# One head pair's output weights loaded in three pieces on a four-engine split, and smaller edits of loads and order, in a one-core decode kernel

## The chip, the cores and the metric

The kernel runs on one core of one Trainium2 chip. A core has TensorE (PE, matrix products; PEld is its weight load), VectorE (DVE), ScalarE (ACT), GpSimd (POOL), SyncE (SP, which here only issues transfers), and 16 DMA engines that move data from the chip's memory (HBM) into the on-chip memory. The engines run side by side and wait for one another by semaphores. The metric is device time of one execution in microseconds (us), lower is better; it is the median of several executions. One more execution was recorded by the hardware profiler, and all rows below come from it.

## The reference

One decode step of a block with adaptive layer norms: four sequences (B = 4), one token each, width 512, all in float32. `c` gives six modulation terms; attention reads caches of 4096 keys and values for 8 key heads (four query heads each); then an MLP over a token axis of length 1 with 1792 hidden units.

```python
mod = (silu(c) @ w_mod).reshape(4, 6, 1, -1)
sa, ca, ga, sb, cb, gb = (mod[:, i] for i in range(6))
h = layernorm(x) * (1 + ca) + sa
x = x + ga * attention(h, k_cache, v_cache, wq, wo)   # softmax(q k^T / sqrt(128)) v, then @ wo
h = layernorm(x) * (1 + cb) + sb
x = x + gb * mixer(h, w1, b1, w2, b2)                 # w2 . gelu(w1 h + b1) + b2 for each channel
```

The inputs are 157 MB, nearly all of it keys and values, and each byte is used once.

## The kernel before, in words

**Units.** There are 32 units, one for each (sequence, key head) pair. Unit i needs a key tile (128 rows, 16 KB each, 2 MB in all) and a value tile of the same size. For each unit PE makes the scores (`scores`, L221), DVE their row maximum, PE and DVE turn it and spread it over the rows, ACT takes the exponential (L251), DVE transposes the probabilities, PE multiplies them with the values (`values`, L281), the groups are picked and scaled (`pick`, `copy_o`), and the result goes through the unit's output weights (`project`, L332) into an accumulator per sequence.

**Loads.** All input loads are issued by SP in program order. `load_pair(i)` (L166) loads the keys of unit i + 2 and the values of unit i in one transfer of 4 MB into a ring of three slots (`tag="kv"`); it waits until the slot that it overwrites has been read. The output weights lie in four tiles of two heads each, `wo_p[0]` to `wo_p[3]`, each 128 rows of 16 KB, loaded by `load_wo` (L171) at the start and in the iterations 1, 3 and 5 of the main loop. `load_wm24` (L175, L176) loads three of the modulation matrices in two transfers, `load_wm5` the sixth at the end. The last unit's values come by `load_v` in pieces: a list `cuts` gives the column blocks (32 blocks `j` of 128 numbers per row) at which a piece ends. A transfer of 128 rows is shared among the 16 DMA engines.

**Order.** The engines run their instructions in the order in which the program issues them (`manual_schedule`). For units 0 to 23 a loop sets it; for the last eight units it is written out by hand, in `PLAN`, one word a step: `v31.2` is the third part of the last unit's value products, `z31` the last two column blocks of them (L299), `a31`, `A31`, `p31` pick, scale and project it. The words that start with z are the end of the last sequence: statistics of the attention's result (`zs`), their gathering over the rows by a product with ones (`zg`, L372 and L377), modulation (`zm`), broadcast (`zb0`, `zb1`, L411) and normalisation (`zn`).

**Mixer.** For each sequence a `Mixer` expands the normalised row to 14 blocks `js` (DVE, L425), applies gelu (ACT, L481) and contracts them with `w2` (`contract_wide`, L436: one block uses one strip of 32 of PE's columns, so that four blocks use all four strips). Sequence 2's mixer runs beside the last eight units; two of its last contractions (`c`) stand in the plan after the gather of the last sequence. The last sequence's own mixer is `finish` (L527): ACT and DVE alternate over the 14 blocks, PE contracts each, and in between PE makes the last gate (`modmm`, L199) from the sixth modulation matrix in four steps k, of which step 0 is made by `zw0` ahead of it.

Lines that set the places:

```python
cuts = {NS - 1: (0, 16, 24, 28, 30, 32), NS - 2: (0, 16, 32)}
last, halves = [(0, 1, 2, 3), (4, 5), (6,), (7,)], [(0, 1), (2, 3), (4, 5), (6, 7)]
... E x v31.0 f v31.1 v31.2 v31.3 V31 z31 a31 I A31 p31
zs g zq zg T2 c zx c zm zq zb0 T3 zg zb1 zw0 zn zc
```

`WIDE` (L24) says how many copies of the four picked columns `pick` writes for units 27 and 28: a product with 4 x that many columns of which only four are used.

Of the kernel before, what the change touches and what calls it, by code (L numbers as in the profile page):

```python
# [14 lines left out]
B, D, HQ, HKV, SK, DH, F = 4, 512, 32, 8, 4096, 128, 1792  # L15
REP = HQ // HKV
NF = F // 128
EPS = 1e-5
P = 128
NS = B * HKV  # L20
NSM = 3 * NF + 16 + 1


WIDE = {NS - 5: 24, NS - 4: 32}  # L24
NARROW = NS - 3


@with_exitstack
def adaln_decode(ctx: ExitStack, tc: tile.TileContext, small, x, wmod, wq, kk, kv, vv, wo, out):
    nc = tc.nc  # L30
    pad = ctx.enter_context(tc.tile_pool(name="pad", bufs=1))
    ring = ctx.enter_context(tc.tile_pool(name="ring", bufs=3))
# [13 lines left out]
    sm = cst.tile([P, NSM], F32, name="sm")  # L46
    xr = wk.tile([P, D], F32, name="xr", tag="yw", bufs=1)[0:B]
    wm01 = ring.tile([P, 2, 4, D], F32, name="wm01", tag="kv")
    nc.sync.dma_start(wm01, wmod[0])
    nc.sync.dma_start(sm, small)  # L50
    nc.sync.dma_start(xr, x)
    wqt = []
    for k in range(0, 4, 2):
        t = ring.tile([P, 2, HQ * DH], F32, name=f"wq{k}", tag="kv")
# [28 lines left out]
    wo_p = [wos.tile([P, 2, REP, D], F32, name=f"wo{h}") for h in range(0, HKV, 2)]  # L83
# [65 lines left out]
    def slots():  # L149
        return ring.tile([P, 2, SK], F32, name="kv", tag="kv")  # L150
# [17 lines left out]
        value(t[:, 1], i)  # L168

    def load_wo(h):  # L170
        nc.sync.dma_start(wo_p[h // 2], wo[h // 2])  # L171

    def load_wm24():
        w = ring.tile([P, 3, 4, D], F32, name="wm24", tag="kv")
        nc.sync.dma_start(w[:, 0:2], wmod[1])  # L175
        nc.sync.dma_start(w[:, 2], wmod[2][:, 0])  # L176
        for e in range(3):
            WM[2 + e] = w[:, e]

    def load_wm5():  # L180
        t = slots().rearrange("p s (k n) -> p (s k) n", n=D)
        nc.sync.dma_start(t[:, 0:4], wmod[2][:, 1])
        WM[5] = t[:, 0:4]
        return t[:, 4:6]

# [10 lines left out]
    def modmm(pm, t, ks=range(4)):  # L196
        for k in ks:
            for c in range(4):
                mm(pm[32 * c:32 * c + 32, :], sT8[:, k].rearrange("p b r -> p (b r)"),  # L199
                   WM[t][:, k, c * P:(c + 1) * P], start=(k == 0), stop=(k == 3))  # L200
# [107 lines left out]
    def pick(i):  # L308
        po = PV.pop(i)
        n, m = po.shape[-1] // DH, WIDE.get(i, 1)  # L310
        if i in OT:
# [38 lines left out]
    def fold_groups(pool, acc, tag):  # L350
        pc = pool.tile([P, P], F32, name="pc", tag=tag)
        for c in range(4):
            mm(pc[32 * c:32 * c + 32, :], first, acc[:, c * P:(c + 1) * P], start=True, stop=True)
        return pc
# [68 lines left out]
    def expand(u, hb, wr, js):  # L423
        for e, j in enumerate(js):
            dv.tensor_scalar(u[:, e, :], hb, wr[:, j:j + 1], b1[:, j:j + 1], op0=OP.mult, op1=OP.add)  # L425

    def contract(py, u, js):
        for e, j in enumerate(js):
            for c in range(4):
                mm(py[32 * c:32 * c + 32, :], w2[:, j:j + 1].to_broadcast([P, 32]),  # L430
                   u[:, e, c * P:(c + 1) * P], start=(j == 0), stop=(j == NF - 1))

    def contract_wide(py, u, js):
        for e, j in enumerate(js):
            q = j % 4
            mm(py[32 * q:32 * q + 32, :], w2[:, j:j + 1].to_broadcast([P, 32]), u[:, e, :],  # L436
               start=(j < 4), stop=(j >= NF - 4))

    class Mixer:
# [48 lines left out]
        def consume(self, most=9):  # L488
# [3 lines left out]
                (contract_wide if self.wide else contract)(self.py, u, js)  # L492
            del self.done[:most]

        def gather_up(self):
            yw = wk.tile([P, D], F32, name="yw", tag="yw", bufs=1)
            dv.tensor_copy(yw, self.py)
            self.py = fold_groups(ps_e, yw, "e")
# [27 lines left out]

    def finish(b, pg, py, hb, wr):  # L527
        uu = ring.tile([P, 16, D], F32, name="uu", tag="kv")
        for js in ((0,), (1,), (2, 3, 4), (5, 6, 7), (8, 9, 10), (11, 12), (13,)):
            j = js[0]  # L530
            if j < 2:
                nc.scalar.activation(uu[:, j], hb, AF.Gelu_apprx_tanh, bias=b1[:, j:j + 1], scale=wr[:, j:j + 1])
                u = uu[:, j:j + 1]
            else:
                u = uu[:, j:j + len(js)]
                expand(u, hb, wr, js)
                nc.scalar.activation(u, u, AF.Gelu_apprx_tanh)  # L537
            contract(py, u, js)
            if j == 1:
                modmm(pg, 5, (1, 2, 3))  # L540
        mix.close()
        dv.tensor_mul(osb[:, :B - 1], ZK, pg.unsqueeze(1).to_broadcast([P, B - 1, P]))
        dv.tensor_add(osb[:, :B - 1], osb[:, :B - 1], XK[:, :B - 1])
        gbl = cst.tile([P, P], F32, name="gbl")
        dv.tensor_copy(gbl, pg)
        dst = out.rearrange("b (c n) -> b c n", c=4)
        for e in range(B - 1):
            (nc.scalar if e == B - 2 else nc.sync).dma_start(dst[e], osb[8 * e:P:32, e])
        dv.scalar_tensor_tensor(osb[:, b], py, b2, gbl, op0=OP.add, op1=OP.mult)
        dv.tensor_add(osb[:, b], osb[:, b], XK[:, b])  # L550
        nc.sync.dma_start(dst[b], osb[8 * b:P:32, b])
# [15 lines left out]
    load_first()  # L567
    load_pair(0)
    load_wo(0)
    for i in range(2):  # L570
        for step in (scores, row_max, turn_max, col_max, spread_max, copy_max, expo):
# [3 lines left out]
    mix = None  # L575
    for i in range(NS - HKV):
        load_pair(i + 1)
        if i in (1, 3, 5):
            load_wo(i + 1)
        if i == 1:  # L580
            load_wm24()
# [17 lines left out]
        if i and i % HKV == 0:  # L599
            mix = Mixer(i // HKV - 1)  # L600
# [14 lines left out]
        if i == NS - HKV - 2:  # L615
# [4 lines left out]
    mix, row = Mixer(B - 2), Mixer(B - 1)  # L620
    pve = pgx = pc = ep = spare = slot = None
    gates = list(range(2 * REP))
    cuts = {NS - 1: (0, 16, 24, 28, 30, 32), NS - 2: (0, 16, 32)}
    last, halves = [(0, 1, 2, 3), (4, 5), (6,), (7,)], [(0, 1), (2, 3), (4, 5), (6, 7)]
    PLAN = """
    a23 v24.0 A23 p23 t25.0 P23 F R v24.1 LP25 G s26 t25.1 M H V24 LP26 Q a24 S26 v25.0 N s27 x A24 f p24 g
    x LP27 m26 S27 P24 m27 X26 X27 b26 B26 e26 x b27 v25.1 c g t26.1 l25 t26.0 B27 s28 V25 c g L25
# [1 line left out]
    LK30 t27.1 S29 P26 v27.0 m29 l27 g LK31 T t28.1 X29 LT t28.0 s30 L27 S30 b29 v27.1 B29 e29 l28 m30 V27  # L629
    LV28 L28 a27 g X30 t29.1 t29.0 l29 L29 s31 A27 LV29 b30 p27 x B30 S31 c c m31 e30 P27 X31 v28.0 f LT LV30  # L630
    b31 v28.1 B31 f e31 LV31 l30 V28 L30 t30.1 l31 L31 a28 t31.1 A28 p28 v29.0 v29.1 t30.0 f P28 V29 v30.0 a29
    v30.1 A29 LW p29 f v30.2 v30.3 t31.0 P29 g V30 Y y a30 A30 p30 E x v31.0 f v31.1 v31.2 v31.3 V31 z31 a31 I A31 p31
    zs g zq zg T2 c zx c zm zq zb0 T3 zg zb1 zw0 zn zc
    """
    TABLE = {"s": scores, "S": row_max, "m": turn_max, "X": col_max, "b": spread_max, "B": copy_max, "e": expo,
             "l": sums, "L": scale, "V": copy_v, "a": pick, "A": copy_o, "P": add_up,
             "LP": load_pair}
    MIX = {"F": mix.fold, "R": mix.residual, "G": mix.gather, "M": mix.modulate, "H": mix.gather, "Q": mix.spread,
           "N": mix.normalise, "g": mix.gelu, "c": lambda: mix.consume(1), "zc": mix.gather_up, "zq": row.gather_eps,
           "zg": row.gather,  # L640
           "zm": row.modulate, "zn": row.normalise}
    for step in PLAN.split():
        op, k = step.rstrip("0123456789."), step.lstrip("abcdefghijklmnopqrstuvwxyzABCDEFGHIJKLMNOPQRSTUVWXYZ")
# [22 lines left out]
        elif op == "LV":  # L666
            load_v(slot[:, i % 2], i, cuts.get(i, (0, 32)))
        elif op == "LW":
            spare = load_wm5()
        elif op == "x":  # L670
            mix.expand(spare if mix.n == 6 else None)
# [24 lines left out]
        elif op == "zb":  # L696
            if i == 0:
                py = ps_s.tile([P, 8, P], F32, name="py3", tag="s")
            row.spread(py[:, 4:], (2 * i, 2 * i + 1))
    finish(B - 1, pgx[:, 0], py[:, 0], row.hb, row.wr)  # L700


# [32 lines left out]
```

## Time and profile before

| | |
|---|---|
| median of 3 timed executions | 387.23 us (387.15 to 387.37) |
| the profiled execution | 387.3 us, of which the span shown is 385.2 |
| busy share: PE, DVE, ACT, POOL | 77%, 51%, 29%, 2% |
| loaded from HBM | 157.32 MB |
| mean granted clock of TensorE | 0.892 |

A row of the timeline gives start and duration in us, the engine, the kernel's line, the operation, output<-inputs by the program's names, shapes, how many, and in brackets how long the engine had been idle and which engine and line ended that. A row of the chain of waits gives start, duration and what the end was waiting for. L numbers are lines of the kernel before. A DMA share of 1.00 means that all 16 engines were busy.

### The profile page before, as it was taken

How to read it: one execution, taken by the hardware profiler on the slowest of the kernel's cores; microseconds unless marked ns; L12 is line 12 of the kernel's file. 1: busy time of each engine (PE TensorE's matmuls, PEld its weight loads, DVE VectorE, ACT ScalarE, POOL GpSimd, SP SyncE). 2: the span in 40 equal slices, each digit the busy share in tenths (PEclk: the TensorE clock that was granted, in tenths of full speed). 3: DMA queues.
4: the chain of work that ended last, by engine and by line, in shares of the span. 5: the costliest groups of instructions: out<-in, count | busy, mean ns of one | idle time of the engine just before them, and what ended most of it. 6: DMA issues, size and time to landing. Idle time of an engine off the chain costs nothing.

```text
span 385.2 us, 5574 instructions
## 1 busy us (share of the span) xinstructions
PE 295.1 (77%) x2376; PEld 116.2 (30%) x2376; DVE 195.4 (51%) x386; ACT 111.5 (29%) x141; POOL 8.5 (2%) x30
## 2 busy tenths in 40 slices
PE   0865778865856939879877868799777897999984
PEld 0111122311223303334322322343222353344653
DVE  0120252620442614664766545648665566788756
ACT  1001111121110111112567211115674103758166
POOL 1200000000000000000000000000000000000000
PEclk9998555985995886998999998989999998999999
DMA  8999999999999999999999999999999999999920
GB/s 331 436 436 436 407 456 436 407 439 429 423 444 432 424 436 432 434 436 434 436 435 436 434 433 430 425 429 427 432 434 432 430 432 424 432 423 427 416 101 3
DMA packets 7408, 157.68 MB, mean 409 GB/s; under 512 B 964, under 2 KB 1236, under 8 KB 1496
## 3 DMA queue, kind: packets, MB, share of 16 engines
q1 hardware_dynamic: 7376, 157.33, 95.2%
q8 instruction: 18, 0.29, 0.3%
q14 instruction: 6, 0.05, 0.0%
q10 hardware_dynamic: 8, 0.00, 0.0%
HBM read 157.32 MB, written 0.01 MB: 408 GB/s over the span
## 4 chain that ended last, share of the span: by engine, by line
DMA 54%; PE 32%; DVE 8%; ACT 4%; issue 1%; POOL 1%; SPq 0%; ACTq 0%
DMA kv<-in_kv 42%; PE s L221 10%; PE pv L281 7%; DMA wm<-in_wmod 5%; DMA kv<-in_kk 4%; DVE m L226 3%; PE s L113 2%; DVE p L257 2%; DMA sm<-in_small 2%; PE pa L332 2%; PE pt L318 1%; PE pb L241 1%; ACT uu L537 1%; PE pm L205 1%; PE pve L293 1%; PE pm L230 1%
## 5 line engine op out<-in xcount | busy, mean ns | idle before, releaser
L221 PE MATMUL s<-kv,QT 128*32 128x512 f32 x512 | 79.0, 745 | 42.1 <-DMA kv<-in_kv 38.5
L226 DVE TENSOR_REDUCE m<-s 128x1 f32<-128x1024 f32 x32 | 39.2, 1224 | 101.9 <-PE s L221 101.7
L251 ACT ACTIVATE p<-s,nm 128x1024 f32<-128x1024 f32 x32 | 35.6, 1114 | 182.7 <-DVE nm L246 182.6
L281 PE MATMUL pv<-kv,p 128*32 128x512 f32 x464 | 67.1, 646 | 0.5 <-DMA kv<-in_kv 0.5
L221 PEld LDWEIGHTS s<-kv,QT 128*32 128x32 f32 x512 | 16.5, 126 | 88.5 <-DMA kv<-in_kv 54.8
L318 PEld LDWEIGHTS pt<-g,po 128*128 128x128 f32 x236 | 30.4, 200 | 28.5 <-issue 21.2
L332 PE MATMUL pa<-wo,oT 128*32 128x512 f32 x240 | 33.6, 633 | 4.6 <-DVE oT L324 4.5
L318 PE MATMUL pt<-g,po 128*128 128x4 f32 (+2 forms) x236 | 33.1, 264 | 1.5 <-DVE po L304 1.0
L257 DVE STREAM_TRANSPOSE p<-p 128x1024 f32<-128x1024 f32 x25 | 30.8, 1233 | 0.0
L304 DVE COPY po<-pv 128x512 f32<-128x512 f32 x29 | 20.0, 688 | 15.5 <-PE pv L281 15.5
L235 DVE TENSOR_REDUCE mx<-pm 1x128 f32<-1x512 f32 x32 | 21.3, 669 | 1.1 <-PE pm L230 1.1
L425 DVE TENSOR_SCALAR u<-hb,wr,sm 128x512 f32<-128x512 f32 x40 | 19.9, 539 | 1.9 <-POOL wr L420 1.0
L481 ACT ACTIVATE u<-u 128x1024 f32<-128x1024 f32 x20 | 20.4, 1051 | 1.5 <-DVE u L425 1.4
L251 ACT ACT_TABLE_LOAD x11 | 14.1, 1283 | 20.4 <-DVE nm L246 20.4
L348 DVE TENSOR_TENSOR acc<-acc,pa 128x512 f32<-128x512 f32 x26 | 17.8, 686 | 3.1 <-PE pa L332 3.1
L241 PEld LDWEIGHTS pb<-neg,mx 1*128 1x128 f32 x64 | 10.0, 194 | 26.9 <-DVE mx L235 25.2
L113 PE MATMUL s<-wm,sT 128*4 128x512 f32 x16 | 9.0, 725 | 11.3 <-DVE sT L99 11.3
L481 ACT ACT_TABLE_LOAD x13 | 16.7, 1283 | 0.2
L281 PEld LDWEIGHTS pv<-kv,p 128*32 128x32 f32 x464 | 13.3, 146 | 6.2 <-issue 2.3
L230 PE MATMUL pm<-ident,m 128*1 128x128 f32 x32 | 9.2, 286 | 7.6 <-DVE m L226 3.5
L241 PE MATMUL pb<-neg,mx 1*128 1x1 f32 x64 | 12.7, 265 | 2.1 <-DVE mx L235 2.1
L436 PE MATMUL py<-u,sm 128*32 128x512 f32 x80 | 13.5, 593 | 0.4 <-ACT u L481 0.4
(134 smaller groups left out, 207.9 us busy)
## 6 DMA issues: line engine op xcount, KB each, us to landing
kv<-in_kv SPq DMA_DIRECT2D x28, 4096.0 KB, 21.9
wq<-in_wq SPq DMA_DIRECT2D x2, 4096.0 KB, 16.2
wo<-in_wo SPq DMA_DIRECT2D x4, 2048.0 KB
kv<-in_kv SPq DMA_DIRECT2D x4, 2048.0 KB, 19.5
wm<-in_wmod SPq DMA_DIRECT2D x2, 2048.0 KB, 14.4
kv<-in_kk SPq DMA_DIRECT2D x1, 4096.0 KB
kv<-in_vv SPq DMA_DIRECT2D x3, 1024.0 KB
wm<-in_wmod SPq DMA_DIRECT2D x1, 1024.0 KB
```

The costliest lines, as they stand in the source:

```text
L221: mm(s[32 * c:32 * c + 32, n * 512:(n + 1) * 512], QT[:, b, h, :], KT[i][:, (n * 4 + c) * 512:(n * 4 + c + 1) * 512], start=True, stop=True)
L226: dv.tensor_reduce(M[i], S[i], axis=AX.X, op=OP.max)
L235: dv.tensor_reduce(mx, M[i].rearrange("o (c r) -> o r c", c=4).unsqueeze(1).to_broadcast([1, 4, 32, 4]), axis=AX.X, op=OP.max)
L241: mm(pb, M[i].rearrange("o c r -> o (c r)"), neg1, start=True, stop=True)
L251: nc.scalar.activation(p, S[i], AF.Exp, bias=M.pop(i), accum_out=l)
L257: dv.transpose(PL[i][0], PL[i][0])
L281: mm(PV[i][32 * q:32 * q + 32, :], pT[:, 128 * k:128 * k + 128:4], VT[i][:, 4 * k:4 * k + 4, :].rearrange("p j d -> p (j d)"), start=(k < ...
L304: dv.tensor_copy(PV[i], pv)
L318: mm(pt, po[:, c * DH:(c + 1) * DH], sel.unsqueeze(1).to_broadcast([P, m, REP]), start=(c == 0), stop=(c == n - 1))
L332: mm(pa[32 * g:32 * g + 32, :], oT[:, g:g + 1].to_broadcast([P, 32]), wo_t[h][:, g, :], start=True, stop=True)
L425: dv.tensor_scalar(u[:, e, :], hb, wr[:, j:j + 1], b1[:, j:j + 1], op0=OP.mult, op1=OP.add)
L481: nc.scalar.activation(u, u, AF.Gelu_apprx_tanh)
```

## The change

Four groups of edits. (1) The third tile of output weights, `wo_p[2]`, is loaded by three transfers: the first 14 KB of each of the 128 rows, then the last 2 KB of the rows 0 to 123, then the last 2 KB of the rows 124 to 127. The host lays the weights out in four arrays for that. (2) Three modulation matrices come in one transfer in place of two, and the last unit's values in four pieces in place of five: the blocks 24 to 27 and 28, 29 are one piece, and their products one step. (3) Of sequence 2's remaining contractions the first block is made by a new step `k` ahead of the last sequence's first gather. (4) `finish` makes step 1 of the gate product ahead of its first contraction, and `pick` writes 32 copies for unit 27 in place of 24.

```diff
-WIDE = {NS - 5: 24, NS - 4: 32}
+LONG = 2 * 4 * 512 - 512
+WIDE = {NS - 5: 32, NS - 4: 32}
...
     def load_wo(h):
-        nc.sync.dma_start(wo_p[h // 2], wo[h // 2])
+        if h != HKV - 4:
+            nc.sync.dma_start(wo_p[h // 2], wo[h // 2] if h < HKV - 4 else w6)
+            return
+        flat = wo_p[h // 2].rearrange("p e g n -> p (e g n)")
+        nc.sync.dma_start(flat[:, :LONG], ws)
+        for lo, hi in ((0, P - 4), (P - 4, P)):
+            nc.sync.dma_start(flat[lo:hi, LONG:], wl[lo:hi])
 
     def load_wm24():
         w = ring.tile([P, 3, 4, D], F32, name="wm24", tag="kv")
-        nc.sync.dma_start(w[:, 0:2], wmod[1])
-        nc.sync.dma_start(w[:, 2], wmod[2][:, 0])
+        nc.sync.dma_start(w, wm2)
...
+        def consume_one(self):
+            u, js = self.done[0]
+            contract_wide(self.py, u, js[:1])
+            self.done[0] = (u[:, 1:], js[1:])
...
     def finish(b, pg, py, hb, wr):
         uu = ring.tile([P, 16, D], F32, name="uu", tag="kv")
+        modmm(pg, 5, (1,))
...
             if j == 1:
-                modmm(pg, 5, (1, 2, 3))
+                modmm(pg, 5, (2, 3))
...
-    cuts = {NS - 1: (0, 16, 24, 28, 30, 32), NS - 2: (0, 16, 32)}
-    last, halves = [(0, 1, 2, 3), (4, 5), (6,), (7,)], [(0, 1), (2, 3), (4, 5), (6, 7)]
+    cuts = {NS - 1: (0, 16, 24, 30, 32), NS - 2: (0, 16, 32)}
+    last, halves = [(0, 1, 2, 3), (4, 5), (6, 7)], [(0, 1), (2, 3), (4, 5), (6, 7)]
...
-    zs g zq zg T2 c zx c zm zq zb0 T3 zg zb1 zw0 zn zc
+    zs g zq k zg T2 c zx c zm zq zb0 T3 zg zb1 zw0 zn zc
...
+    wm = a["w_mod"].reshape(4, P, 6, D).transpose(1, 2, 0, 3)
+    w = a["A_wo"].reshape(HKV // 2, 2, REP, DH, D).transpose(0, 3, 1, 2, 4)
+    wf = w[HKV // 2 - 2].reshape(P, -1)
...
+        "ws": con(wf[:, :LONG]),
+        "wl": con(wf[:, LONG:]),
```

What stands on the engines. First SP's queue of loads before, from the second tile of output weights on (`wo_121` is `wo_p[1]`, `wm_316` the three modulation matrices, then rows x numbers per row):

```order
L171 DMA wo_121<-in_wo 128x4096
L175 DMA wm_316<-in_wmod 128x4096
L176 DMA wm_316<-in_wmod 128x2048
L166 DMA kv<-in_kv 128x8192 x2
L171 DMA wo_122<-in_wo 128x4096
```

And SP's queue at that place with the change:

```order
L173 DMA wo_121<-in_wo 128x4096
L182 DMA wm_316<-in_wm 128x6144
L167 DMA kv<-in_kv 128x8192 x2
L176 DMA wo_122<-in_ws 128x3584
L178 DMA wo_122<-in_wl 124x512
L178 DMA wo_122<-in_wl 4x512
```

One transfer of 4096 numbers a row has become one of 3584 and two of 512, of 124 and of 4 rows; nothing has moved past another load. SP's last value loads before:

```order
L194 DMA kv<-in_vv 128x1024
L194 DMA kv<-in_vv 128x512
L194 DMA kv<-in_vv 128x256 x2
```

And with the change:

```order
L200 DMA kv<-in_vv 128x1024
L200 DMA kv<-in_vv 128x768
L200 DMA kv<-in_vv 128x256
```

The piece of 512 and the first of 256 have become one. Last, PE from the last projection on, before (`pgx` is the attention's result, `pst` the gathered statistics, `py<-u` and `py<-kv` sequence 2's contractions, `py_2385<-h` the broadcast):

```order
L337 MATMUL pgx<-wo_123,oT 32x128 x16
L372 MATMUL pst<-epsr,ones 128x24
L377 MATMUL pst<-stm,ones 128x24
L436 MATMUL py<-u,sm 32x512 x2
L436 MATMUL py<-kv,sm 32x512 x2
L372 MATMUL pst<-epsr,ones 128x24
L411 MATMUL py_2385<-h_2374,ident 128x128 x2
```

And PE there with the change:

```order
L343 MATMUL pgx<-wo_123,oT 32x128 x16
L378 MATMUL pst<-epsr,ones 128x24
L442 MATMUL py<-u,sm 32x512
L383 MATMUL pst<-stm,ones 128x24
L442 MATMUL py<-u,sm 32x512
L442 MATMUL py<-kv,sm 32x512 x2
L378 MATMUL pst<-epsr,ones 128x24
L417 MATMUL py_2385<-h_2374,ident 128x128 x2
```

One of the four products of 512 columns has moved ahead of the gather (L383, before L377), which waits for DVE's `stm`.

More of the change, by code (lines that the diff above doesn't have):

```diff
@@ L21, with adaln_decode @@
 NSM = 3 * NF + 16 + 1
-WIDE = {NS - 5: 24, NS - 4: 32}
+LONG = 2 * 4 * 512 - 512
+WIDE = {NS - 5: 32, NS - 4: 32}
 NARROW = NS - 3
 @with_exitstack
-def adaln_decode(ctx: ExitStack, tc: tile.TileContext, small, x, wmod, wq, kk, kv, vv, wo, out):
+def adaln_decode(ctx: ExitStack, tc: tile.TileContext, small, x, wm0, wm2, wm5, wq, kk, kv, vv, wo, w6, ws, wl, out):
     nc = tc.nc
@@ L48, in adaln_decode @@
     wm01 = ring.tile([P, 2, 4, D], F32, name="wm01", tag="kv")
-    nc.sync.dma_start(wm01, wmod[0])
+    nc.sync.dma_start(wm01, wm0)
     nc.sync.dma_start(sm, small)
@@ L181, in load_wm5 @@
         t = slots().rearrange("p s (k n) -> p (s k) n", n=D)
-        nc.sync.dma_start(t[:, 0:4], wmod[2][:, 1])
+        nc.sync.dma_start(t[:, 0:4], wm5)
         WM[5] = t[:, 0:4]
@@ L631, in adaln_decode @@
     b31 v28.1 B31 f e31 LV31 l30 V28 L30 t30.1 l31 L31 a28 t31.1 A28 p28 v29.0 v29.1 t30.0 f P28 V29 v30.0 a29
-    v30.1 A29 LW p29 f v30.2 v30.3 t31.0 P29 g V30 Y y a30 A30 p30 E x v31.0 f v31.1 v31.2 v31.3 V31 z31 a31 I A31 p31
-    zs g zq zg T2 c zx c zm zq zb0 T3 zg zb1 zw0 zn zc
+    v30.1 A29 LW p29 f v30.2 v30.3 t31.0 P29 g V30 Y y a30 A30 p30 E x v31.0 f v31.1 v31.2 V31 z31 a31 I A31 p31
+    zs g zq k zg T2 c zx c zm zq zb0 T3 zg zb1 zw0 zn zc
     """
@@ L638, in adaln_decode @@
     MIX = {"F": mix.fold, "R": mix.residual, "G": mix.gather, "M": mix.modulate, "H": mix.gather, "Q": mix.spread,
-           "N": mix.normalise, "g": mix.gelu, "c": lambda: mix.consume(1), "zc": mix.gather_up, "zq": row.gather_eps,
+           "N": mix.normalise, "g": mix.gelu, "c": lambda: mix.consume(1), "k": mix.consume_one, "zc": mix.gather_up, "zq": row.gather_eps,
            "zg": row.gather,
@@ L719 @@
         "x": con(a["A_x"].reshape(B, D)),
-        "wmod": con(a["w_mod"].reshape(4, P, 3, 2, D).transpose(2, 1, 3, 0, 4)),
+        "wm0": con(wm[:, 0:2]),
+        "wm2": con(wm[:, 2:5]),
+        "wm5": con(wm[:, 5]),
         "wq": con(a["A_wq"].reshape(2, 2, P, HQ * DH).transpose(0, 2, 1, 3)),
@@ L724 @@
         "vv": con(v[NS - 2:]),
-        "wo": con(a["A_wo"].reshape(HKV // 2, 2, REP, DH, D).transpose(0, 3, 1, 2, 4)),
+        "wo": con(w[:HKV // 2 - 2]),
+        "w6": con(w[-1]),
+        "ws": con(wf[:, :LONG]),
+        "wl": con(wf[:, LONG:]),
     }
```

## The prediction, made before the changed kernel was run

> **What bounds the kernel now.** First the page: its span, the DMA lines, the queues and the chain of what ended last.
>
> ```profile
> span 385.2 us, 5574 instructions
> ...
> DMA  8999999999999999999999999999999999999920
> ...
> q8 instruction: 18, 0.29, 0.3%
> ...
> DMA 54%; PE 32%; DVE 8%; ACT 4%; issue 1%; POOL 1%; SPq 0%; ACTq 0%
> ```
>
> The 16 DMA engines are full in every slice but the first and the last two. So until about 367 us the end is set by when bytes land, and after that by a serial chain. The end of the chain of waits, in order of time (start, duration, what), shows the seam:
>
> ```profile
> 365.67 1.91 PE pve L293 x60
> 367.63 0.58 PE pt L299 x4
> 368.21 0.22 PE pt L312 x2
> 368.43 0.33 PE pgx L685 x2
> 368.76 1.05 PE pgx L337 x32
> 369.83 0.31 DVE st L365
> ...
> 375.87 4.11 ACT uu L537 x3
> 379.99 1.05 ACT uu L537
> ```
>
> L299 needs the very last piece of the values; from there on nothing runs beside the chain that could absorb a delay. Did the data or PE set the start of L299? The rows of weight loads, with what ended the idle time before them, and the issue of the values:
>
> ```profile
> 362.46 0.81 PEld L293 LDWEIGHTS pve<-kv,p 128*32 128x32 f32 x32 [0.85 <-DMA kv<-in_vv]
> 367.14 0.14 PEld L293 LDWEIGHTS pve<-kv,p 128*32 128x32 f32 x4 [0.18 <-DMA kv<-in_vv]
> 367.60 0.52 PEld L299 LDWEIGHTS pt<-p,kv 128*128 128x128 f32 x4 [0.31 <-PE pve L293]
> 346.45 6.58 SPq L194 DMA_DIRECT2D kv<-in_vv  x7
> ```
>
> PE waits for data at 362.46 and at 367.14, and L299 starts 0.46 us after the latter. The loads were issued by 353, some 14 us before the last is used, so the issue is not late: the DMA engines are the pace. Then, how many of them? The stretches (PE, PEld, DVE, ACT, POOL busy; clock; DMA share; GB/s):
>
> ```profile
> 366.20:366.40 0.20, 0.20 (x20) 0.20 (x12) 0.20 (x1) 0.20 (x1) 0.00 (x0) 1.00 1.27 502
> 367.20:367.80 0.60, 0.53 (x10) 0.29 (x6) 0.20 (x1) 0.58 (x2) 0.00 (x0) 1.00 0.58 246
> 368.40:369.00 0.60, 0.60 (x15) 0.48 (x18) 0.16 (x1) 0.35 (x2) 0.00 (x0) 1.00 0.58 246
> 369.60:370.00 0.40, 0.40 (x10) 0.29 (x2) 0.17 (x1) 0.00 (x0) 0.00 (x0) 1.00 0.00 0
> ```
>
> From 367.2 to 369.0 the share stands at 0.58, which is 9 of 16 engines: seven have finished everything and nine are a whole 1 MB load (2.4 us) behind. A load has landed when its slowest engine has. **So what counts is not the bytes in all but the bytes and delays of the latest engine.**
>
> Who is late, the views do not say, but the packets behind them do: the trace holds start, length and size of each, and every engine closes its share of a load with a 4-byte packet. Sixteen such marks per load, in us after the first; * are the four engines that took the four rows of `xr` (packets of 2048 bytes at 7.631, 7.824, 7.841 and 7.875, each followed at once by that engine's next load, which fixes its place among the sixteen):
>
> ```
> load ending at  46.4: 0.000 0.014 0.028 0.046 0.074* 0.213 0.222 0.267* 0.278 0.285* 0.319* 0.354 0.371 0.399 0.531 0.601
> load ending at 102.1: 0.000 0.028 0.046 0.074* 0.213 0.267* 0.277 0.284* 0.319* 0.354 0.370 0.530 0.601 1.433 1.641 1.819
> load ending at 107.0: 0.000 0.028 0.046 0.074* 0.213 0.267* 0.278 0.319* 0.354 0.371 0.531 0.601 1.131* 1.433 1.641 1.819
> load ending at 286.1: 0.000 0.184 0.238* 0.290* 0.502 0.572 0.601* 1.391 1.438 1.669 1.747 1.756 1.945* 2.824 3.032 3.205
> last load, late nine: 369.178* 369.202 369.215 369.235 369.423 369.479 369.552 369.565 369.596
> ```
>
> The places keep to 10 ns until one engine jumps. Jumps of 1.42 us come with each of the 18 packets of q8 (instruction fetches), in turn on eight engines that are none of the four. One starred engine jumps three times by 0.85 (107, 228 and 324 us) with no packet recorded; it happens after 58, 195 and 320 of DVE's instructions, so I take it for DVE's own fetches and expect it again, since DVE's order is the same. Another starred one jumps 0.55 once. So **three of the four are 2.6 to 3.0 us early at the end, and the fourth is one of the nine late ones, only 0.42 us ahead of the latest** (369.178 against 369.596).
>
> **The output weights in three loads.** The same packets give the price: on one engine 16 KB packets start 0.608 us apart, 8 KB 0.306, 2 KB 0.080, 1 KB 0.042, and a mark takes 0.006: about 4 ns plus 38 ns per KB. The shapes that the trace shows are these:
>
> ```profile
> wo<-in_wo SPq DMA_DIRECT2D x4, 2048.0 KB
> xr<-in_x SPq DMA_DIRECT2D x1, 8.0 KB
> kv<-in_vv SPq DMA_DIRECT2D x2, 128.0 KB, 18.4
> wm<-in_wmod SPq DMA_DIRECT2D x1, 1024.0 KB
> ```
>
> Loads of 128 rows have sixteen marks, 8 rows to an engine; `xr`, 4 rows, has four engines with one row each. Equal whole shares in both. 124 is 4 x 31, so equal shares on at most 16 engines mean four engines with 31 rows; the 4 rows go to four as well. That 124 rows use the same four as 4 rows is my choice between the two shown cases; the other end is sixteen engines, as for 128 rows.
> - Every engine: 8 packets of 14 KB in place of 16 KB: 8 x (0.608 - 0.533) = -0.60 us.
> - The four: 31 + 1 packets of 2 KB and two marks: 32 x 0.080 + 0.012 = +2.56, net +1.96 us.
>
> The Trainium skill ("DMA: Bandwidth & Descriptors", "Why a DMA increments its semaphore by 16 and not by 1") has a transfer use the largest number of engines up to 16 that divides its slowest dimension, the lowest-numbered ones: 4 for 124. [...] No row here shows a transfer of 124 rows.
>
> **Fewer pieces.** Three modulation terms in one load and the last values in four: per engine 16 packets and two marks fewer, 16 x 4 + 2 x 6 ns = -0.08 us on all sixteen.
>
> So the twelve gain 0.68, the four lose 1.88. The late starred engine, 0.42 ahead of the old last, ends 1.88 - 0.42 = **1.46 us after it**; the other three, 2.6 and more ahead, end 0.7 ahead or earlier, like the twelve. The engine never runs dry (the 14 us above), so the last landing moves by +1.46, and with it every landing after the fourth weight load, L293's at 362.46 too. Bounds: -0.68 (no late engine among the four) to +1.96.
>
> **The last values in four pieces.** 24 to 29 now land together, 0.35 us (8 x 0.042 + mark) before 30 and 31. Before, PE had done 24 to 27 by then and started 28 and 29 at 367.14, ending with the second pass (0.13 later, 0.27 long) at 367.55, just as the last piece came. Now all six stand between that landing and L299: 0.11 and 0.13 us more passes. I take **+0.2** (0 to +0.3).
>
> **`k` ahead of the gather.** PE's and its neighbours' rows:
>
> ```profile
> 369.70 0.40 PE L372 MATMUL pst<-epsr,ones 1*128 1x24 f32 x2
> 370.40 0.40 PE L377 MATMUL pst<-stm,ones 128*128 128x24 f32 x2 [0.31 <-DVE stm L367]
> 370.74 0.62 PE L436 MATMUL py<-u,sm 128*32 128x512 f32 x2
> 371.19 0.60 PE L436 MATMUL py<-u,sm 128*32 128x512 f32 x2
> 371.66 0.35 DVE L403 SCALAR_TENSOR_TENSOR h<-a,ye,prep 128x128 f32<-128x128 f32 x1
> 371.73 0.29 PEld L372 LDWEIGHTS pst<-epsr,ones 1*128 1x128 f32 x2 [0.84 <-issue]
> 372.13 0.52 PEld L411 LDWEIGHTS py<-h,ident 128*128 128x128 f32 x4
> ```
>
> A strip (32 columns) starts 0.34 after the narrow pair before it (370.40 to 370.74), its second pass 0.45 later, and the next full-width row 0.53 after that (371.20 to 371.73). One strip row between L372 and L377 thus starts at 369.70 + 0.34 = 370.04, its second pass at 370.49, and L377 at 371.02 in place of 370.40: +0.62. The hole there is 0.31 us, the row takes 0.9: four strips side by side take no longer than one, so splitting them saves nothing behind. L411 waits for h (372.01, 0.12 before it), which moves with L377; PE is then free at about 372.7, as late as h. Queued behind L377 are `mv`, `ye`, `h` and the whole end. I take **+0.6** (0, if PE runs a full-width row beside a strip, to +0.65).
>
> **At no cost.** The wider pick, 96 to 128 columns, and the gate product moved up:
>
> ```profile
> 347.29 1.13 PE L318 MATMUL pt<-g,po 128*128 128x96 f32 x8 [0.46 <-DVE rl L270]
> 356.06 1.16 PE L318 MATMUL pt<-g,po 128*128 128x128 f32 x8
> 375.22 0.16 PEld L430 LDWEIGHTS py<-uu,sm 128*32 128x32 f32 x8 [1.06 <-ACT uu L532]
> 377.39 0.59 PEld L430 LDWEIGHTS py<-uu,sm 128*32 128x32 f32 x24 [0.65 <-ACT uu L537]
> ```
>
> +0.03 us fifteen us before the wait of 0.85 at 362.46 that swallows it. The four rows of L199 (0.42 us) fit in the 1.06 us that PE waits for ACT before 375.22, and what they leave behind only lengthens the wait before 377.39. Uncovered, they would cost 0.03 and 0.3. Two more issues on SP, 0.4 us each, stand behind a queue 14 us deep.
>
> **Sum.** The profiled execution took 387.3 (span 385.2 and 2.1 around it), 0.07 over the median of 387.23. 387.3 + 1.46 + 0.2 + 0.6 = 389.56, so **389.5** for the median, +0.6%.
>
> **Rivals.**
> - *The four are light* (not slower): the unrecorded jumps belong to the execution and not to the program, or the engine that has them is not one of the four. Then the latest is one of the twelve and the landing moves by -0.68; with +0.2 and +0.6 this gives 387.3 (same), and 386.7 if `k` hides as well. It decides where the starred late engine has over 1.9 + 0.7 = 2.6 us of slack. For it: three of the four have that. Against: the jumps recur on one engine at about equal counts of DVE's instructions, and the mark at 369.178.
> - *All sixteen share the 124 rows*: no engine changes by more than 0.1; the piece, `k` and -0.08 remain: 387.9.
> - *`k` costs nothing*, the engines as forecast: 388.9.
>
> **Chances.** Forecast 0.52, `k` free 0.14, sixteen engines 0.12, four light with `k` paid 0.12, four light and more gained 0.10. About 0.2% (0.8 us: under 386.5, over 388.0) is what a measurement of this kernel can tell from no change. Slower takes the first two and half of the third: 0.72; same the other half, the fourth and 0.02 of the fifth: 0.20; faster 0.08. The likeliest case alone is 389.0 to 390.0; to leave out no more than 2 in 10 the range reaches from the light case with `k` paid to the upper bound of the DMA term: 387.2 to 390.1.
>
> **What would show it.** Right: in the last microseconds of loading the DMA share falls to 0.06 (one engine) instead of 0.58; the last wait of L293 or L299 for `in_vv` ends near 369; L377 starts 1.3 us after L372 instead of 0.7, and L372 to the end is 0.6 longer. Wrong: L299 at or before 367.5 (the engines balance), or L377 right behind DVE's `stm` with the strip beside it.

## The result, and the profile after

| | median (lowest to highest) |
|---|---|
| before, five executions | 387.23 us (386.96 to 387.41) |
| after, five executions | 390.80 us (390.65 to 391.08) |
| ratio after / before | 1.0092, 95% interval 1.0081 to 1.0103 |

The change makes the kernel slower by 3.6 us. The direction was forecast, the size was not: 390.8 lies 0.7 us above the range. The profiled executions differ by 3.4 us: a span of 388.6 where before it was 385.2.

From the page of the profile after (span, DMA share in tenths and GB/s in 40 slices):

```profile
span 388.6 us, 5574 instructions
...
DMA  8999999999999999999999999999999999999900
GB/s 328 432 432 432 427 435 432 438 424 438 429 386 438 430 432 435 430 432 430 432 428 432 430 433 435 430 430 432 430 432 435 430 432 428 423 431 422 397 28 3
```

The DMA line looks as before: full up to the end. The GB/s line has a dent that the share doesn't have: the twelfth slice (from 106.9 us on) stands at 386 among values around 430. That is where the output weights of the three loads come in. The engines count as busy there, and moved less.

The end of the kernel after, rows of the timeline (start, duration, engine, line, operation; L299, L305, L343, L378, L383, L442 are L293, L299, L337, L372, L377, L436 of before):

```profile
369.83 0.36 PEld L299 LDWEIGHTS pve<-kv,p 128*32 128x32 f32 x12 [0.40 <-DMA kv<-in_vv]
370.39 0.52 PEld L305 LDWEIGHTS pt<-p,kv 128*128 128x128 f32 x4 [0.20 <-issue]
...
372.51 0.40 PE L378 MATMUL pst<-epsr,ones 1*128 1x24 f32 x2
372.83 1.04 PE L442 MATMUL py<-u,sm 128*32 128x512 f32 x2
373.81 0.40 PE L383 MATMUL pst<-stm,ones 128*128 128x24 f32 x2
```

Three differences from the rows of before make up the whole change:

- The last wait for values (in both kernels for the piece that ends with block 29) is over at 369.83 in place of 367.14: **+2.69 us**.
- From there to the start of L305 (L299 before) 0.56 us pass in place of 0.46: +0.10.
- From L378 to L383 1.30 us pass in place of 0.70: +0.60.

They add up to 3.39, and the spans differ by 3.4. The other stretches on the way to the end keep their length within 0.02 us: 2.12 in place of 2.10 from L305 to L378, and 14.8 in both from L383 on.

Which engines were late? The marks of the last load, that of the sixth modulation matrix behind the values (the packets behind the views; starts in us, as in the prediction):

```
before, late nine: 369.18* 369.20 369.22 369.24 369.42 369.48 369.55 369.56 369.60
after, latest ten: 369.74 369.80 369.86 369.91 369.92 369.95 369.98 370.06 370.16 370.26 ... 372.25*
```

After, fifteen engines are through by 370.26, and one is alone for 1.99 us. The stretches of the profile after show it too (length, busy time of PE, PEld, DVE, ACT, POOL, clock, DMA share, GB/s):

```profile
370.50:372.00 1.50, 1.50 (x28) 1.38 (x32) 0.45 (x2) 0.96 (x2) 0.00 (x0) 1.00 0.06 27
```

A share of 0.06 is one engine of 16. The marks say which one. There are 813 of them in place of 837: two loads of sixteen marks are gone and two of four have come, so 124 rows go to four engines, as the 4 rows do. The four that turn from packets of 14 KB to packets of 2 KB have the places 0.255, 0.410, 0.460 and 1.225 in the load of 14 KB. These are the places of the four that took `xr` in this execution, the last of them after its first jump (0.351 before it); followed from mark to mark, that one is the lone one at the end. So the late engine is the forecast one. But it is later than forecast by 3.07 - 1.88 = 1.19 us, and the other fifteen, which were to finish 0.68 earlier (the three other starred ones were early anyway), finish 370.26 - 369.60 = 0.66 **later**. Something held up the late engine and the others alike, by some 1.2 to 1.3 us. Where, shows one stretch of 24 us, of before:

```profile
102.00:126.00 24.00, 14.95 (x96) 5.75 (x95) 8.05 (x14) 2.41 (x4) 0.00 (x0) 0.76 1.01 436
```

and of after:

```profile
102.00:126.00 24.00, 15.86 (x97) 5.35 (x94) 7.62 (x13) 2.41 (x4) 0.00 (x0) 0.71 1.01 411
```

The engines count as busy in both (a share of 1.01), but after they move 25 GB/s less: 24 x 25 / 436 = **1.38 us** of loading lost, by estimate. Most of it lies in six of these microseconds, before:

```profile
106.00:112.00 6.00, 5.28 (x41) 2.16 (x37) 4.21 (x8) 1.16 (x2) 0.00 (x0) 1.00 1.03 445
```

and after:

```profile
106.00:112.00 6.00, 5.63 (x49) 2.01 (x39) 4.28 (x7) 0.43 (x2) 0.00 (x0) 0.98 1.08 368
```

(A row counts a packet whole where it starts, so rows of a single microsecond swing in both kernels and say little.) In this time packets of 32 KB on other engines take up to 2.05 us, where 1.21 is usual, and those of 2 KB up to 0.158, where 0.084 is usual. This is the **hold-up**, and the experiments ask what it comes from.

### The profile page after: what moved, and what is told of

Its sections match the earlier page's. It is cut to its first block, busy times and chain, and to the rows that moved or that the text cites. A ratio compares the mean times of both kernels' runs of the same rounds, so it can differ in the third digit from the quotient of the medians.

```text
span 388.6 us, 5574 instructions
## 1 busy us (share of the span) xinstructions
PE 303.5 (78%) x2376; PEld 119.5 (31%) x2376; DVE 195.8 (50%) x386; ACT 111.5 (29%) x141; POOL 8.6 (2%) x30
## 4 chain that ended last, share of the span: by engine, by line
DMA 55%; PE 31%; DVE 9%; ACT 2%; POOL 1%; issue 1%; SPq 0%; POOLq 0%; ACTq 0%
DMA kv<-in_kv 37%; PE s L227 9%; PE pv L287 8%; DMA wm<-in_wm 6%; DMA kv<-in_vv 5%; DMA kv<-in_kk 5%; DVE m L232 3%; PE s L114 2%; DMA sm<-in_small 2%; DVE p L263 2%; PE pa L338 2%; PE pt L324 2%; PE pb L247 1%; ACT uu L549 1%; PE pm L211 1%; PE pm L236 1%
## 5 line engine op out<-in xcount | busy, mean ns | idle before, releaser
L227 PE MATMUL s<-kv,QT 128*32 128x512 f32 x512 | 76.0, 720 | 37.6 <-DMA kv<-in_kv 34.1
L287 PE MATMUL pv<-kv,p 128*32 128x512 f32 x464 | 71.7, 687 | 0.1
L324 PEld LDWEIGHTS pt<-g,po 128*128 128x128 f32 x236 | 32.7, 214 | 28.1 <-issue 18.3
L338 PE MATMUL pa<-wo,oT 128*32 128x512 f32 x240 | 37.1, 694 | 4.1 <-DVE oT L330 4.0
L324 PE MATMUL pt<-g,po 128*128 128x4 f32 (+1 forms) x236 | 35.5, 274 | 1.5 <-DVE po L310 1.0
L442 PE MATMUL py<-u,sm 128*32 128x512 f32 x80 | 15.3, 613 | 0.0
```

The lines of the kernel that those rows point to most:

```text
L227: mm(s[32 * c:32 * c + 32, n * 512:(n + 1) * 512], QT[:, b, h, :], KT[i][:, (n * 4 + c) * 512:(n * 4 + c + 1) * 512], start=True, stop=True)
L287: mm(PV[i][32 * q:32 * q + 32, :], pT[:, 128 * k:128 * k + 128:4], VT[i][:, 4 * k:4 * k + 4, :].rearrange("p j d -> p (j d)"), start=(k < ...
L324: mm(pt, po[:, c * DH:(c + 1) * DH], sel.unsqueeze(1).to_broadcast([P, m, REP]), start=(c == 0), stop=(c == n - 1))
L338: mm(pa[32 * g:32 * g + 32, :], oT[:, g:g + 1].to_broadcast([P, 32]), wo_t[h][:, g, :], start=True, stop=True)
```

## Experiments

Twelve kernels were run, in three groups of four, each beside the kernel before on its chip (medians 387.31, 387.33 and 387.35). "Split" is edit (1) of the change. For three that are read as slower (the tile whole; 93 + 32 + 3 rows; the column as 112 + 16 rows) the interval of the ratio includes 1: what is said of these rests on their traces together with their medians.

**1 and 2. The split alone, and the same pieces with 128 rows each.** The first takes only edit (1) into the kernel before, the second loads the last 2 KB of all 128 rows at once:

```diff
-        for lo, hi in ((0, P - 4), (P - 4, P)):
+        for lo, hi in ((0, P),):
             nc.sync.dma_start(flat[lo:hi, LONG:], wl[lo:hi])
```

> The kernel before with the three-piece weight load alone (14 KB of 128 rows, then 2 KB of 124 and of 4 rows). Theory A (the pieces put 49 KB more on four engines, one of which has no slack, and hold all sixteen up by 1.3 us while they run): +2.7 us, and one engine's last mark 2 us or more behind the other fifteen. Theory B (the cost is in the pieces as such, not in who carries them): also about +2.7, but the marks of the other engines stand as late as that one.

> The kernel before with the third weight tile in two pieces, 14 KB and 2 KB of all 128 rows each. Theory A: the sixteen engines share it as before, within 0.1 us of the kernel before, no stretch of low DMA rate near 108 us. Theory B: a piece more costs most of what the three pieces cost, +1.5 or more.

Measured: the split alone 390.69 us, ratio 1.0086 (1.0072 to 1.0100); with 128 rows 387.42, ratio 1.0007 (0.9998 to 1.0016). In the split alone fifteen engines are through the last load by 370.63 and one is alone until 373.05, as in the change. Its stretch and its last wait for values:

```profile
102.00:126.00 24.00, 12.28 (x85) 3.95 (x81) 5.73 (x12) 2.41 (x4) 0.00 (x0) 0.79 1.01 402
```

```profile
370.61 0.14 PEld L300 LDWEIGHTS pve<-kv,p 128*32 128x32 f32 x4 [0.18 <-DMA kv<-in_vv]
371.04 0.52 PEld L306 LDWEIGHTS pt<-p,kv 128*128 128x128 f32 x4 [0.29 <-PE pve L300]
```

And with 128 rows in the second piece:

```profile
102.00:126.00 24.00, 18.05 (x119) 6.16 (x115) 10.14 (x18) 2.41 (x4) 0.00 (x0) 0.78 1.02 436
```

```profile
367.25 0.14 PEld L300 LDWEIGHTS pve<-kv,p 128*32 128x32 f32 x4 [0.22 <-DMA kv<-in_vv]
```

The rate is back at 436, and the wait ends at 367.25 (before: 367.14). So neither 14 KB packets nor 2 KB packets nor one more load costs anything that shows; the cost is in the division into 124 and 4 rows.

**3 and 4. The change with the third tile loaded whole, and the change without `k`.**

```diff
 def load_wo(h):
-        if h != HKV - 4:
...
+        nc.sync.dma_start(wo_p[h // 2], wo[h // 2])
```

```diff
-    zs g zq k zg T2 c zx c zm zq zb0 T3 zg zb1 zw0 zn zc
+    zs g zq zg T2 c zx c zm zq zb0 T3 zg zb1 zw0 zn zc
```

> The changed kernel with its third weight tile loaded whole again, all other edits kept. If the strip ahead of the gather costs 0.6 and the longer last piece 0.2 as forecast, +0.7 us over before (387.9); L299's counterpart within 0.3 us of where it is before. If those edits are covered, 387.2.

> The changed kernel without the step k (the strip stays behind the gather). By the forecast 0.6 us less than the changed kernel: +2.9 over before (390.2). If the strip was covered: as the changed kernel, +3.5.

Measured: tile whole 388.11, ratio 1.0012 (0.9990 to 1.0035); without `k` 390.30, ratio 1.0079 (1.0066 to 1.0093). Rows of the chain of waits with the tile whole (start, duration, what):

```profile
367.81 0.54 PE pt L299 x4
...
369.93 0.33 PE pst L372 x2
370.25 0.97 PE py L436 x2
371.23 0.33 PE pst L377 x2
371.56 0.99 PE py L436 x6
```

L377 stands 1.30 us behind L372, with `k`'s strip as the step between them, and DVE no longer on the chain there. Without `k` the timeline has the old hole again:

```profile
372.88 0.40 PE L378 MATMUL pst<-epsr,ones 1*128 1x24 f32 x2
373.59 0.40 PE L383 MATMUL pst<-stm,ones 128*128 128x24 f32 x2 [0.31 <-DVE stm L373]
```

0.71 us apart, as before. By these rows `k` costs 0.6 wherever it is; the times agree (0.5 less without it), though their intervals overlap with that of the change. All edits but the split cost 0.8 us by the medians (388.11 against 387.31).

**5 to 7. How many engines carry the long rows.** The same 2 KB column in three loads whose shares fall on one, two or three of the engines (31 + 96 + 1 rows, 62 + 64 + 2, 93 + 32 + 3). The packets of the first show it: one engine carries 38 of them, the others 6.

```diff
-        for lo, hi in ((0, P - 4), (P - 4, P)):
+        for lo, hi in ((0, 31), (31, 127), (127, 128)):
```

> The kernel before, the last 2 KB of the third tile's rows as 31, 96 and 1 rows. 31 and 1 share equally only on one engine: it carries 38 packets of 2 KB (+2.4 us), the others 6 (-0.1). Theory A (one of four engines is late and has no slack, three have 2.6 us or more): 3 chances in 4 that this engine is a light one, then +0.0 to +0.4; if it is the late one, +2 to +2.5. Theory C (the loss grows with the rows sent to few engines, whoever carries them): +0.8, a quarter of the split's +3.4.

> The same as 62, 64 and 2 rows: two engines carry 36 packets of 2 KB each (+2.3 us), the others 4 (-0.3). Theory A: the full loss of about +2.5 in one step as soon as the late engine is among the two, under +0.8 before that. Theory C: +1.7, half of the split's loss.

> The same as 93, 32 and 3 rows: three engines carry 34 packets of 2 KB each (+2.1 us), the others 2 (-0.4). Theory A: the step has come here or comes only with the fourth engine; with it about +2.9, without it under +1. Theory C: +2.5.

Measured: one engine 388.58 us, ratio 1.0034 (1.0003 to 1.0064); three engines 388.56, ratio 1.0025 (0.9998 to 1.0053). With two engines the times spread from 388.69 to 397.08 (median 390.85, ratio 1.0062, 1.0018 to 1.0105): nothing is built on it. Loaded on one engine:

```profile
102.00:126.00 24.00, 15.45 (x106) 5.48 (x106) 8.21 (x15) 2.41 (x4) 0.00 (x0) 0.74 1.00 411
```

```profile
368.18 0.14 PEld L300 LDWEIGHTS pve<-kv,p 128*32 128x32 f32 x4 [0.17 <-DMA kv<-in_vv]
```

On three:

```profile
102.00:126.00 24.00, 12.75 (x88) 4.53 (x87) 6.66 (x12) 2.41 (x4) 0.00 (x0) 0.79 1.01 403
```

```profile
368.37 0.14 PEld L300 LDWEIGHTS pve<-kv,p 128*32 128x32 f32 x4 [0.18 <-DMA kv<-in_vv]
```

Two things come apart here. The lone late engine is gone: the last marks end together, at 370.59 and 370.79, and the wait ends near 368.3 in place of 370.6. So the late one is the engine that four-engine loads use and these don't; this fits the marks of before, by which three of the four had 2.6 us to spare and one 0.42. But the hold-up is still there, 411 and 403 GB/s, and with it about 1.2 us of time, though nothing is late alone. It is a cost of its own, and neither theory had it: the first, without the late engine, allowed at most 0.4 us for one engine and under 1 for three, the other let the loss grow from 0.8 to 2.5, and both kernels lose about 1.2.

**8. Is it the memory side?** The split read from the old layout, in which the 2 KB pieces lie 16 KB apart, in place of an array of its own:

```diff
+        src = wo[h // 2].rearrange("p e g n -> p (e g n)")
+        for lo, hi, c0, c1 in ((0, P, 0, 3584), (0, P - 4, 3584, 4096), (P - 4, P, 3584, 4096)):
+            nc.sync.dma_start(flat[lo:hi, c0:c1], src[lo:hi, c0:c1])
```

> The three-piece load of 14 KB, 124 and 4 rows as in the change, but from the weights as they lay before, so that neighbouring 2 KB pieces are 16 KB apart in HBM. If the hold-up of all sixteen engines comes from reading one contiguous 256 KB block: about 1.3 us less than the split from the packed copy, +2. If it comes from where the rows are written or from the four engines themselves: the same +3.4, with the same stretch of low DMA rate near 108 us.

Measured: 390.53 us, ratio 1.0073 (1.0050 to 1.0096), the same as the split with its own array, and 403 GB/s in the stretch:

```profile
102.00:126.00 24.00, 15.57 (x95) 4.95 (x92) 7.23 (x13) 2.41 (x4) 0.00 (x0) 0.71 1.01 403
```

For the split, where the bytes lie in the source makes no difference.

**9 and 10. Equal shares, but of other rows.** The 2 KB column as 112 and 16 rows, so that each engine carries 7 + 1 rows, 8 as always; and the whole tile (16 KB a row) so:

```diff
-        nc.sync.dma_start(wo_p[h // 2], wo[h // 2])
+        for lo, hi in ((0, 112), (112, P)):
+            nc.sync.dma_start(wo_p[h // 2][lo:hi], wo[h // 2][lo:hi])
```

> The kernel before, the last 2 KB of the third tile's rows as 112 and 16 rows: 7 + 1 rows on each of sixteen engines if they share equally, so no engine carries more than another. If the hold-up of the 124-row piece comes from which rows an engine writes (7 or 31 neighbouring rows instead of the 8 that it has of a 128-row load): low DMA rate near 108 us and about +1.1 us. If it comes from four engines carrying what sixteen should: no stretch of low rate, +0.1.

> The same with the whole 16 KB rows: the third tile as 112 and 16 rows, eight times the bytes of the run with 112 rows of 2 KB, on sixteen engines. If it matters which rows an engine writes: eight times that run's loss, +5 us or more. If it matters that few engines carry the bytes: +0.1.

Measured: the column 388.58 us, ratio 1.0020 (0.9998 to 1.0041), with 418 GB/s in the stretch and the wait's end at 368.09:

```profile
102.00:126.00 24.00, 16.26 (x110) 5.74 (x106) 9.23 (x16) 2.41 (x4) 0.00 (x0) 0.83 1.01 418
```

The whole tile 393.64, ratio 1.0146 (1.0102 to 1.0190). Its stretches:

```profile
102.00:126.00 24.00, 12.19 (x84) 4.07 (x84) 6.73 (x12) 2.41 (x4) 0.00 (x0) 0.71 1.02 336
...
106.00:108.00 2.00, 2.00 (x20) 0.36 (x12) 0.69 (x1) 0.36 (x2) 0.00 (x0) 1.00 1.01 266
108.00:110.00 2.00, 1.78 (x18) 1.35 (x18) 1.75 (x3) 0.00 (x0) 0.00 (x0) 1.00 1.24 238
110.00:112.00 2.00, 1.84 (x17) 0.30 (x9) 2.00 (x4) 0.00 (x0) 0.00 (x0) 1.00 1.20 246
```

Here is the hold-up at full length: with the same bytes on each engine as in the kernel before, the sixteen engines count as busy throughout and move 238 to 266 GB/s in place of 436. 24 x 100 / 436 = 5.5 us are lost in the stretch, 6.3 in the time. The balance of the engines is not its cause; that the rows of a load fall on the engines in another way than in a load of 128 rows is what all the slow kernels have in common and the one of 128 rows hasn't. This is argued from what they share; why it slows them, no run shows.

**11. Are the unrecorded jumps DVE's fetches?** 128 more DVE copies in the iterations 4 to 7 of the kernel before:

```diff
+        if i in (4, 5, 6, 7):
+            for _ in range(32):
+                dv.tensor_copy(half2, half)
```

> The kernel before with 128 more DVE copies of one column in the iterations 4 to 7 of the main loop, 32 in each. If the late one of the four engines is late by the fetches of DVE's instructions: its jumps of 0.85 us come at the same counts of DVE's instructions as before, so four of them instead of three before the last values, it ends 0.4 us behind the latest other engine, +0.3 to +0.5 us. If the jumps belong to something else (a clock, the bytes): three jumps at the old times, 387.3.

Measured: 390.96 us, from 387.46 to 393.86, ratio 1.0056 (1.0019 to 1.0093). The profiled execution is the longest of these, and in it the copies hold DVE up so far that no packet starts from 171.0 to 174.1. So the time answers nothing, but the packets do. The jumps of that engine begin with a pause of 0.30 us, and the data packet behind it takes some 0.54 us more (one of 32 KB 1.75 in place of 1.21). Before there are three, at 103.3, 228.3 and 323.5 us, when DVE has started about 59, 195 and 321 instructions. With the copies there are four, at 105.0, 155.5, 233.3 and 327.4 us, at about 58, 186, 319 and 447 instructions. The two before the standstill are on the same engine, whose place goes from 0.194 to 1.031 and from 0.859 to 1.714. So the additional jump comes 128 of DVE's instructions after the first, as expected if they are DVE's fetches: the jumps go with DVE's instruction count. That what is fetched are instructions is still inferred.

**12. The four pieces of the last values alone.**

```diff
-    cuts = {NS - 1: (0, 16, 24, 28, 30, 32), NS - 2: (0, 16, 32)}
+    cuts = {NS - 1: (0, 16, 24, 30, 32), NS - 2: (0, 16, 32)}
```

> The kernel before with the last unit's values in four pieces instead of five, nothing else. By the forecast +0.2 us (0 to +0.3), L299 0.2 later behind the last wait for data; if PE's products of the longer piece are covered, -0.05.

Measured: 387.45 us, ratio 0.9991 (0.9971 to 1.0011).

```profile
367.42 0.36 PEld L293 LDWEIGHTS pve<-kv,p 128*32 128x32 f32 x12 [0.56 <-DMA kv<-in_vv]
367.99 0.52 PEld L299 LDWEIGHTS pt<-p,kv 128*128 128x128 f32 x4 [0.20 <-issue]
```

0.57 us from the wait's end to L299 in place of 0.46: the same +0.1 as in the change.

No kernel here beat the one before.

## Why the prediction was wrong in size

Step by step, against the change's own rows:

| step of the prediction | forecast | measured |
|---|---|---|
| last landing later | +1.46 | +2.69 |
| last values in four pieces | +0.2 | +0.10 |
| `k` ahead of the gather | +0.6 | +0.60 |
| sum on the profiled execution | +2.26 | +3.39 |

**What held.** That the end is set by the latest engine and not by the bytes; that 124 rows go to the four engines of `xr` (chosen between two shown cases, and borne out by the marks after), of which the fourth is a late one; that it ends alone, with a share of 0.06; that one strip of four costs as much as four and pushes the gather by 0.6; that the wider pick, the gate product and the merged modulation loads are hidden: the tile-whole kernel has them all and is 0.8 us above before, of which `k` and the cuts account for 0.7. The four's surplus over the rest nearly held too: the late engine moved by 3.07 us and the latest of the rest by 0.66, which is 2.41 apart; the step said 1.88 + 0.68 = 2.56 (32 x 0.080 + 0.012 is 2.57, not 2.56; the slip changes nothing). The Trainium skill's rule of the largest divisor ("DMA: Bandwidth & Descriptors", "Why a DMA increments its semaphore by 16 and not by 1") gives four engines for 124 rows, and the four marks of that load agree.

**What failed** is the step "The four: 31 + 1 packets of 2 KB and two marks" with its conclusion "So the twelve gain 0.68, the four lose 1.88". The packets of 14 KB kept their price, mostly 0.53 us apart. But the step priced the 2 KB packets, and left all others, at the time that they take in a stream of 128-row loads, and took the sixteen engines as independent. They are not while such a load runs: the late engine lost a further 1.19 us, and the latest of the rest ended 0.66 later instead of 0.68 earlier, 1.34 apart. Forecast plus hold-up, 1.46 + 1.2, is about the measured +2.69. For the same reason the upper bound of +1.96 was no bound: it held only the four engines' own packets at their undisturbed price.

The trace of before could not have shown the hold-up, since all its large loads have 128 rows and its one load of 4 rows moves 8 KB. A sound bound would have said so: an operation that the trace lacks can also cost others something.

**What stays open.** Why those rows are slow. A reading that would fit, and that no run shows, is that in loads of 128 rows every engine always writes rows of its own, and that after another split two engines write into the same rows, or the same part of the on-chip memory, and wait for one another; the runs show only that it depends on the row counts and not on the source, the packet size or the balance. Nor is it settled why the split alone lands later (370.61) than the whole change (369.83), which makes the split (+3.4) and the rest (+0.8) add up to more than the measured 3.6; the two other kernels with 124 and 4 rows lie between (370.20 and 370.23). One of them is the change without `k`, whose loads are those of the change: so 0.37 us of this can come from one profiled execution to another, and the hold-up is known no better than that.

## What to carry to other kernels

Keep a large load at 128 rows (or shape its pieces so that each has all 128), and cut it along the columns: cut along the rows it may use few engines, and even with equal shares it slowed all of them here while it ran. Where a kernel is bound by loading, read its end by engine: a DMA share that falls in steps of 1/16 tells how many engines are still at work, and work can only be taken from the latest, so that an engine held to be spare has to be seen to be spare in the marks. Check a busy DMA share against its GB/s; a dent in the second alone says that engines which count as busy are slowed; by what, it doesn't say.

## What was unexpected of the hardware

- A 2 MB load of 112 and 16 rows, 7 + 1 rows to each engine, runs at 238 to 266 GB/s in place of about 436 while all engines count as busy, and costs 6.3 us; 256 KB of it cost 1.2 us.
- Cutting the same tile by columns, 14 KB and 2 KB of 128 rows each, costs nothing that shows (387.42 against 387.31 us).
- One DMA engine pauses by about 0.85 us at about every 128 of DVE's instructions, with no packet recorded: three times before, four times with 128 more DVE instructions.
